# A scan and a mixture of adapters on one core: a small head for the pipeline, 2 KB rows for eight chunks, new order ranks

## The chip, the core and the metric

The kernel runs on one core of a Trainium2 chip. The metric is the device time of one execution in microseconds. The core has a matrix engine (PE, TensorE), three engines for elementwise work (DVE, ACT, POOL), a sequencer that mostly issues transfers (SP), and 16 DMA engines. Each engine works through its own list of instructions in order; semaphores join the lists.

## What is computed

The input `a` and `b` are float32 of shape 8 x 6400 x 128. For each of the 8 sequences a recurrence runs along the 6400 steps; its result `x` (51200 rows of 128) goes through a top-2 mixture of 8 low-rank adapters:

```python
for t in range(S):
    h = a[:, t] * h + b[:, t]
    out[:, t] = h
...
logits = x @ w_gate                    # 128 -> 8
topk = the two largest logits per row
w = softmax over these two
delta = sum over the two of w * (x @ A[e]) @ B[e]   # 128 -> 16 -> 128
return x + delta
```

It reads 52.4 MB and writes 26.2 MB, all in float32. The inner values are kept in float16.

## The kernel before, in words

**Chunks.** The 51200 rows are 100 chunks of 512 rows (four blocks of 128). A chunk passes through a front and a back.

The front of chunk `c`: `load` (L526) brings `a` and `b` into `a_tm` and `b_tm`, six slots of two chunks each; PE transposes both into PSUM (`A`, `B`, or `P`, which interleaves the `b` of one chunk with the `a` of the next); ACT copies `a` to `a_st` (`ae`); DVE runs the scan along 512 steps (`sc`, L613) and leaves `xT`, 128 features by 512 rows in float16. `xT` has 24 slots.

A unit `u` is a run of blocks, six of them up to the last 16 blocks, four from there on. PE multiplies each block with the eight A matrices and the gate weights side by side (`Z`, 136 columns) and ACT copies the result to `zl` (`ze`).

Units form groups. `gating(gi)` takes the logits of a group at once: maximum (`g1`, DVE), difference, mask and second maximum, sigmoid of the difference (`w1`, ACT) and the masked weights (`g8`, DVE). The five wide steps between run on POOL (`q2`, `q3`, `q5`, `q6`, `q7`), in the last six groups on DVE (`WIDE_DVE`). A group has four units, 24 blocks or six chunks; the last eight units form groups of 2, 2, 1, 1, 1, 1 (`TAPER`). There are 21 groups.

The back of a chunk needs the gates of its whole group: multiply `zl` with the gates (`mu` on POOL, or `md` on DVE for the chunks in `MU_DVE`, counted from the end), four transposes on PE (`T`), a copy out of PSUM (`te`, on DVE, on ACT for one chunk in six), then two matmuls per block that add `x` transposed back and the adapters' output (`D`), a copy to `outt` (`oe`, ACT), and the store. Stores go out for two chunks at a time, the last four for one.

**Rows of a load.** `paired(c)` (L523) chooses between two layouts. Unpaired, a partition holds four successive rows of a chunk (2 KB), and the chunk is transposed with four matmuls over all 128 partitions for each of `a` and `b`. Paired, a partition holds eight successive rows of two chunks (4 KB); each chunk then lies in one half of the partitions and takes eight transposes of 64 rows, and those of `a` and `b` alternate between the halves of the array. The first eight chunks (`HEAD`) are unpaired and come one at a time in 256 KB loads, all others are paired and come in 512 KB loads for two chunks.

**Order.** Nothing of the order is written by hand. Each operation gets a rank: a base from the number of its chunk, unit or group, plus `TEMPLATE[kind][place in the period of six]`, plus `NUDGE[name]` for single operations of the head and the tail. `Program.schedule` (L208) then plays the program with modelled durations. An engine that comes free takes, among the operations whose rank lies within `WINDOW[engine]` of its lowest, the one that could start first. The order so found is the order of the instruction list of each engine; `waits` adds the semaphores. All loads but one and all stores are in SP's list. In the model, `DMA_DEPTH` says that SP can't issue while nine transfers are under way.

**Ends.** For the last 12 chunks (`TAIL_CHUNKS`) the transposes and deltas use the PSUM banks of the front too, once its scans are done (`place`). Two stores, of chunks 56 and 78, are cut into 120 and 8 partitions (`SPLIT`).

Of the kernel before, what the change touches and what calls it, by code (L numbers as in the profile page):

```python
# [15 lines left out]
PE_FREE = 0.1  # L16
Q_RATE = {3: 3.6e-3, 5: 2.1e-3, 7: 2.1e-3}
SCAN_SELF = 0.13
ISSUE = {"sp": 0.52, "act": 0.45}
LOAD_RATE = 392e3  # L20
STORE_RATE = 408e3
# [86 lines left out]
START = (-999, "", 0)  # L108
FIRST = -9999
EARLY = -400  # L110
LEAD = []
TAPER = [2, 2, 1, 1, 1, 1]
WIDE_DVE = [1, 2, 3, 4, 5, 6]
TE_LAST = []
TAIL_UNITS = [4, 4, 4, 4]
TE_ACT = [1]
MU_DVE = [1, 2, 4, 6, 8]
TAIL_CHUNKS = 12
WARM0 = 12
WARM = 16  # L120
HALVES = 0.745
PAIR_RATE = 411e3
HEAD = 8
TAIL = 0
STORE_TAIL = [1, 1, 1, 1]
# [754 lines left out]
```

## Time and profile before

| | us |
|---|---|
| median of 3 runs | 207.19 (206.95 to 208.16) |
| the profiled execution | 207.91 |
| its span, first to last instruction | 205.9 |
| PE busy | 184.7 |
| DVE busy | 177.7 |
| ACT busy | 169.1 |
| POOL busy | 144.6 |

Busy times are sums over the span. Engine names stand before line numbers (L613 is line 613 of the kernel); a tile's name tells the step: `a_tm` and `b_tm` the loads, `pA` and `pB` the transposed inputs, `a_st` the copied `a`, `xT` the scan, `pZ` and `zl` the logits, `m`, `k`, `L`, `sd`, `g` the gate, `zw` the multiply, `zwT` its transpose, `pO` the delta, `outt` the output. A chain row or a wait row reads "waiter <- what it waited for". In a row of a stretch, the numbers are its length, then busy time and count of each engine that worked in it, the granted PE clock, the share of the DMA engines, and GB/s.

### The profile page before, as it was taken

The page shows a single profiled execution, that of the slowest core. Times are in us where ns is not written, and L with a number is a line of the kernel's source. Part 1 is how long each engine was busy: PE and PEld are TensorE (multiplying, and loading weights), DVE is VectorE, ACT ScalarE, POOL GpSimd, SP SyncE. Part 2 cuts the span into 40 slices and gives each one's busy share as a digit, 9 for nine tenths or more (in the row PEclk, how much of TensorE's full clock was granted, in tenths as well). Part 3 has the DMA queues.
Part 4 walks back from the last instruction along what each step waited for, and adds up shares of the span by engine and source line. Part 5 has one row for each costly group of instructions (what it writes and reads, how often), then busy time and mean ns, then how long its engine had stood idle before and what let it go on. Part 6 is the DMA issues. An engine that isn't in the chain of part 4 may idle for free.

```text
span 205.9 us, 7539 instructions
## 1 busy us (share of the span) xinstructions
PE 184.7 (90%) x3152; PEld 160.9 (78%) x3152; DVE 177.7 (86%) x289; ACT 169.1 (82%) x306; POOL 144.6 (70%) x176
## 2 busy tenths in 40 slices
PE   7779589999998899899799999999999999879683
PEld 6557478887897789788689888988888888857572
DVE  0789688998998899798899999999997999989881
ACT  2356668999998999899799999999999998886372
POOL 1000328879898978878788988899989898687420
PEclk9999958999999999999999999999999999999789
DMA  6999999999999999999999999999999999997388
GB/s 191 368 392 415 405 409 406 405 409 405 411 417 406 414 403 417 409 403 416 408 409 400 409 395 408 415 410 411 409 412 410 410 409 404 405 352 289 132 299 300
DMA packets 30559, 79.26 MB, mean 385 GB/s; under 512 B 3774, under 2 KB 3902, under 8 KB 30526
## 3 DMA queue, kind: packets, MB, share of 16 engines
q1 hardware_dynamic: 29054, 78.39, 97.1%
q10 hardware_dynamic: 1472, 0.40, 0.8%
q8 instruction: 25, 0.41, 0.8%
q14 instruction: 8, 0.07, 0.1%
HBM read 52.56 MB, written 26.21 MB: 383 GB/s over the span
## 4 chain that ended last, share of the span: by engine, by line
PE 67%; DVE 12%; DMA 10%; POOL 3%; issue 3%; SPq 2%; ACT 1%; DVEq 0%; POOLq 0%
PE pA L562 14%; PE pB L562 12%; PE pZ L633 11%; PE pO L734 10%; PE pO L720 10%; PE pO L735 9%; DMA a_tm<-in_a_dram 7%; DVE xT L613 5%; DMA b_tm<-in_b_dram 3%; POOL zw L707 3%; SPq L541 2%; DVE zwT L729 2%; DVE zw L711 1%; ACT outt L744 1%; DVE g L688 1%
## 5 line engine op out<-in xcount | busy, mean ns | idle before, releaser
L613 DVE TENSOR_TENSOR_SCAN xT<-a_st,xT,pB 128x512 f16<-128x512 f32 x96 | 120.3, 1253 | 9.5 <-PE pA L562 5.6
L707 POOL TENSOR_TENSOR zw<-zl,g 128x512 f16<-128x512 f32 x95 | 100.4, 1069 | 24.7 <-PE pO L720 11.3
L562 PE MATMUL pB<-ident_f,b_tm 64*128 64x64 f32 (+1 forms) x768 | 71.4, 235 | 6.5 <-DMA a_tm<-in_a_dram 2.8
L580 ACT COPY a_st<-pA 128x512 f32<-128x512 f32 x100 | 60.5, 612 | 17.5 <-PE pA L562 16.0
L562 PE MATMUL pA<-ident_f,a_tm 64*128 64x64 f32 (+1 forms) x768 | 71.7, 235 | 2.0 <-DMA a_tm<-in_a_dram 1.0
L562 PEld LDWEIGHTS pB<-ident_f,b_tm 64*128 64x128 f32 (+1 forms) x768 | 57.9, 142 | 12.5 <-issue 3.7
L562 PEld LDWEIGHTS pA<-ident_f,a_tm 64*128 64x128 f32 (+1 forms) x768 | 57.9, 142 | 8.2 <-DMA a_tm<-in_a_dram 2.3
L639 ACT COPY zl<-pZ 128x816 f32<-128x816 f32 (+1 forms) x68 | 58.0, 853 | 2.3 <-PE pZ L633 1.6
L744 ACT COPY outt<-pO 128x512 f32<-128x512 f32 x92 | 52.7, 609 | 7.7 <-PE pO L735 7.3
L734 PE MATMUL pO<-ident_h,xT 128*128 128x128 f16 x368 | 50.1, 223 | 1.2 <-DVE zwT L729 1.0
L735 PE MATMUL pO<-cst_h,zwT 128*128 128x128 f16 x368 | 48.9, 220 | 0.8 <-issue 0.8
L734 PEld LDWEIGHTS pO<-ident_h,xT 128*128 128x128 f16 x368 | 40.5, 114 | 4.8 <-DVE zwT L729 2.1
L633 PE MATMUL pZ<-cst_h,xT 128*128 128x136 f16 x400 | 36.5, 228 | 1.5 <-DVE xT L613 0.6
L735 PEld LDWEIGHTS pO<-cst_h,zwT 128*128 128x128 f16 x368 | 36.9, 100 | 0.8 <-issue 0.8
L720 PE MATMUL pO<-ident_h,zw 128*128 128x128 f16 x368 | 33.2, 221 | 2.0 <-ACT outt L744 1.3
L729 DVE COPY zwT<-pO 128x512 f16<-128x512 f16 x77 | 30.2, 410 | 3.4 <-PE pO L720 3.1
L633 PEld LDWEIGHTS pZ<-cst_h,xT 128*128 128x128 f16 x400 | 27.1, 115 | 4.4 <-DVE xT L613 1.3
L720 PEld LDWEIGHTS pO<-ident_h,zw 128*128 128x128 f16 x368 | 22.3, 98 | 6.0 <-issue 1.9
L669 POOL TENSOR_TENSOR k<-zl,m 128x192 f32<-128x192 f32 x15 | 7.8, 519 | 22.9 <-DVE m L667 22.9
L671 POOL TENSOR_SCALAR L<-k 128x192 f32<-128x192 f32 x15 | 12.9, 860 | 1.3
L613 DVE TENSOR_TENSOR_SCAN xT<-a_st,pB 128x512 f16<-128x512 f32 (+1 forms) x8 | 7.5, 939 | 4.6 <-PE pB L562 4.3
L678 POOL TENSOR_TENSOR L<-k,m 128x192 f32<-128x192 f32 x15 | 7.9, 524 | 2.8 <-DVE m L676 2.7
(41 smaller groups left out, 106.1 us busy)
## 6 DMA issues: line engine op xcount, KB each, us to landing
a_tm<-in_a_dram SPq DMA_DIRECT2D x46, 512.0 KB, 10.7
b_tm<-in_b_dram SPq DMA_DIRECT2D x46, 512.0 KB, 10.6
out_dram<-outt SPq DMA_DIRECT2D x46, 512.0 KB, 10.8
a_tm<-in_a_dram SPq DMA_DIRECT2D x8, 256.0 KB, 5.8
b_tm<-in_b_dram SPq DMA_DIRECT2D x7, 256.0 KB, 6.0
out_dram<-outt SPq DMA_DIRECT2D x4, 256.0 KB, 2.7
out_dram<-outt SPq DMA_DIRECT2D x2, 480.0 KB
b_tm<-in_b_dram ACTq DMA_DIRECT2D x1, 256.0 KB, 3.6
```

The source lines that it names most:

```text
L562: last = eng["pe"].transpose(*args)
L580: lambda: eng["act"].copy(a_st[c % NA][:, :], pA[:, c % 2, :]), fr(c, "ae"))
L613: last = eng["dve"].tensor_tensor_scan(out=x[:, s0:s1], data0=a_st[c % NA][:, s0:s1], data1=pB[:, c % 2, s0:s1], initial=init, op0=ALU.mul ...
L633: last = eng["pe"].matmul(pZ[:, k // (n // 2), o : o + W], xblock(b0 + k), Awg_h)
L639: return eng["act"].copy(zl[:, zb : zb + n, :].rearrange("p (h k) w -> p h (k w)", h=2), pZ[:, :, 0 : n // 2 * W])
L671: lambda e: e.tensor_scalar(out=ll, in0=kk, scalar1=0.0, scalar2=-1.0e30, op0=ALU.is_ge, op1=ALU.mult), dve=not main)
L707: lambda: eng["pool"].tensor_tensor(out=wv, in0=zv, in1=gv, op=ALU.mult), ba(gi, c, "mu"))
L720: last = eng["pe"].transpose(ptile[:, k * 128 : k * 128 + 128], zw[w][:, k, :], ident_h[:, :])
L729: lambda: eng["dve"].tensor_copy(zwT[w][:, :], ptile[:, 0:C]), ba(gi, c, "te"))
L734: eng["pe"].matmul(dst, xblock(b0 + k), ident_h[:, :], start=True, stop=False)
L735: last = eng["pe"].matmul(dst, zwT[w][:, k * 128 : k * 128 + 128], B_h, start=False, stop=True)
L744: lambda: eng["act"].copy(outt[:, o0 : o0 + n, :].rearrange("p k w -> p (k w)"), bank),
```

## The change

- The first three units are four blocks long, one chunk each (`HEAD_UNITS`), and the groups begin with one of one unit and one of two (`LEAD`). So the gate of chunk 0 needs chunk 0 alone, that of chunks 1 and 2 needs these two, and the groups of six chunks begin with chunk 3.
- At the end one of the two groups of two units goes (`TAPER`). There are 22 groups; the sixth from the end, whose wide steps run on DVE, now is one of 24 blocks.
- Chunks 4 to 11 (pairs 2 to 5, `FLAT`) are loaded two at a time in unpaired rows of 2 KB and transposed over 128 partitions. Chunks 0 to 3 still come one at a time (`HEAD` 4). Before, chunks 4 to 7 were single unpaired loads and 8 to 11 paired.
- The multiplies of the last ten chunks all run on DVE (`MU_DVE`, before five of the last eight), and the PSUM copies `te` of six of the last ten on ACT (`TE_LAST`).
- No store is cut (`SPLIT` is empty).
- In the planner, an operation that waits for a landing, or that is issued by SP, counts its operands as later by a margin when the order is sought (`LAND_MARGIN`, `SP_MARGIN`). Its transfer rates are changed by about 1%, and the windows, the templates and the nudges are all new.

```diff
+SP_MARGIN = 2.0
+LAND_MARGIN = 1.0
...
-LOAD_RATE = 392e3
-STORE_RATE = 408e3
+LOAD_RATE = 387e3
+STORE_RATE = 413e3
...
 NUDGE = {
-    "A0": -158.252, "A1": -127.324, "A2": -123.096, "A3": 32.941, "A4": 44.278, "A5": 34.44, "A6": 59.414, "A7":
...
+    "A0": -7.373, "A1": 6.112, "A10": -1.64, "A11": 34.468, "A12": 1.111, "A2": 15.408, "A3": -24.636, "A4":
...
-WINDOW = {'pe': 16.262, 'act': 17.153, 'dve': 47.02, 'pool': 47.064, 'sp': 57.831}
+WINDOW = {'pe': 42.345, 'act': 35.431, 'dve': 24.751, 'pool': 5.955, 'sp': 63.924}
...
-LEAD = []
-TAPER = [2, 2, 1, 1, 1, 1]
+LEAD = [1, 2]
+TAPER = [2, 1, 1, 1, 1]
 WIDE_DVE = [1, 2, 3, 4, 5, 6]
-TE_LAST = []
+TE_LAST = [1, 2, 4, 6, 8, 10]
 TAIL_UNITS = [4, 4, 4, 4]
+HEAD_UNITS = [4, 4, 4]
+FLAT = [2, 3, 4, 5]
 TE_ACT = [1]
-MU_DVE = [1, 2, 4, 6, 8]
+MU_DVE = [1, 2, 3, 4, 5, 6, 7, 8, 9, 10]
...
-PAIR_RATE = 411e3
-HEAD = 8
+PAIR_RATE = 414.5e3
+HEAD = 4
 TAIL = 0
 STORE_TAIL = [1, 1, 1, 1]
-SPLIT = {56: [120, 8], 78: [120, 8]}
+SPLIT = {}
 TEMPLATE = {
...
-    "sc": [-2.149, -1.286, 6.521, -19.69, -9.638, -0.216],
+    "sc": [-11.65, -1.923, -9.807, -8.205, -4.3, 4.861],
...
-    "oe": [26.926, 32.894, 33.316, 36.556, 35.829, 26.06],
+    "oe": [19.127, 13.522, 10.649, 2.757, 11.757, 27.623],
...
+    def margin(self, d, op):
+        return (SP_MARGIN if op.eng == "sp" else 0.0) + (LAND_MARGIN if d.sem is not None else 0.0)
+
     def schedule(self):
...
-                users[d.i].append((op, self.lag(d, op)))
+                users[d.i].append((op, self.lag(d, op) + self.margin(d, op)))
...
-    for n in [U] * ((NBLK - sum(TAIL_UNITS)) // U) + TAIL_UNITS:
+    for n in HEAD_UNITS + [U] * ((NBLK - sum(HEAD_UNITS) - sum(TAIL_UNITS)) // U) + TAIL_UNITS:
...
         def un(u, kind):
-            return (PERIOD * (u // GMAX), kind, u % GMAX)
+            v = u - len(HEAD_UNITS)
+            if v < 0:
+                return ((units[u][0] + units[u][1] - 1) // J - 1, kind, 0)
+            return (sum(HEAD_UNITS) // J + PERIOD * (v // GMAX), kind, v % GMAX)
...
         def paired(c):
-            return HEAD <= c < NCH - TAIL
+            return HEAD <= c < NCH - TAIL and c // HC not in FLAT
...
-                    q, f"{key}{c}", n * C * D * 4 / (PAIR_RATE if paired(c) else LOAD_RATE),
+                    q, f"{key}{c}", n * C * D * 4 / (PAIR_RATE if paired(c) else STORE_RATE if n == HC else LOAD_RATE),
```

More of the change, by code (lines that the diff above doesn't have):

```diff
@@ L121 @@
 HALVES = 0.745
-PAIR_RATE = 411e3
-HEAD = 8
+PAIR_RATE = 414.5e3
+HEAD = 4
 TAIL = 0
 STORE_TAIL = [1, 1, 1, 1]
-SPLIT = {56: [120, 8], 78: [120, 8]}
+SPLIT = {}
 TEMPLATE = {
-    "la": [-13.284, -13.376, -10.147],
-    "lb": [-12.856, -11.393, -13.112],
-    "A": [3.619, 4.619, -4.264, 6.619, 7.619, 8.619],
-    "B": [-2.245, 2.718, -8.407, 8.99, 6.061, 4.41],
-    "ae": [-1.493, 12.357, 10.831, 7.96, 5.931, 11.772],
-    "sc": [-2.149, -1.286, 6.521, -19.69, -9.638, -0.216],
-    "Z": [6.623, 2.916, -2.696, 9.959],
-    "ze": [6.413, 12.686, 18.636, 4.611],
-    "g1": [1.078],
-    "g2": [15.192],
-    "g3": [12.311],
-    "g4": [-7.624],
-    "g5": [43.586],
-    "g6": [18.91],
-    "w1": [27.261],
+    "la": [-7.837, -6.512, -2.793],
+    "lb": [-6.969, -4.142, -2.441],
+    "A": [-29.85, -22.77, -4.07, -28.889, -8.078, -19.823],
+    "B": [-12.19, -0.608, 4.625, 4.731, 6.492, -13.789],
+    "ae": [13.823, -17.155, -11.299, -7.863, -15.554, -16.07],
+    "sc": [-11.65, -1.923, -9.807, -8.205, -4.3, 4.861],
+    "Z": [-11.931, -1.652, 0.404, 0.668],
+    "ze": [-0.53, 2.002, 2.058, 7.184],
+    "g1": [-5.254],
+    "g2": [6.652],
+    "g3": [-1.394],
+    "g4": [5.837],
+    "g5": [2.097],
+    "g6": [-3.795],
+    "w1": [9.977],
     "w2": [27.183],
@@ L146 @@
     "p3": [35.473],
-    "mu": [22.377, 11.789, 38.051, -6.995, 25.901, 25.822],
-    "T": [17.564, 18.694, 15.643, 19.013, 20.568, 20.925],
-    "te": [11.47, 21.167, 12.791, -1.785, 1.996, 11.732],
-    "D": [13.525, 17.402, 15.169, 14.035, 19.652, 27.901],
-    "oe": [26.926, 32.894, 33.316, 36.556, 35.829, 26.06],
-    "st": [25.679, 26.621, 29.881],
-    "ta": [14.725, 30.746, 16.943, 18.052, 19.161, 20.27],
-    "md": [78.718, -0.018, -87.87, 12.1, 13.209, 14.318],
+    "mu": [7.135, 7.159, 9.752, 13.89, 13.317, 14.36],
+    "T": [8.957, 2.123, 1.909, 11.496, 1.102, -5.077],
+    "te": [5.714, 2.101, 13.025, 13.738, 15.827, 9.439],
+    "D": [11.989, 5.151, 4.181, 3.366, 5.179, -2.649],
+    "oe": [19.127, 13.522, 10.649, 2.757, 11.757, 27.623],
+    "st": [27.717, 29.832, 33.435],
+    "ta": [-17.067, 3.889, 6.417, 53.389, -5.208, -15.308],
+    "md": [14.061, -2.161, 18.001, 16.54, -9.981, -19.458],
     "wu": [-0.198],
-    "ch": [26.813],
+    "ch": [4.744],
     "mb": [0.0],
-    "q2": [17.668],
-    "q3": [-16.399],
-    "q5": [-0.842],
-    "q6": [-2.93],
-    "q7": [1.928],
+    "q2": [-2.296],
+    "q3": [2.325],
+    "q5": [0.245],
+    "q6": [3.55],
+    "q7": [1.073],
     "q8": [35.473],
-    "g7": [47.426],
-    "g8": [9.111],
+    "g7": [-1.33],
+    "g8": [-0.424],
 }
@@ L721, in tr @@
                 return last
-            o_T[c] = P.add("pe", f"T{c}", 0.1 + 0.056 * n, [(o_mu[c], True), (o_ih, True)] + free + [(o, True) for o in o_wu if c < 2], tr, ba(gi, c, "T"))
+            o_T[c] = P.add("pe", f"T{c}", 0.1 + 0.056 * n, [(o_mu[c], True), (o_ih, True)] + free + [(o, True) for o in (o_wu if c < 2 else [])], tr, ba(gi, c, "T"))
             if te_act(c):
```

147 rows, old and new, of the table NUDGE are left out of this document.

## The prediction

> **What bounds the kernel now.** I read the page first, for busy shares and DMA slices.
>
> ```profile
> span 205.9 us, 7539 instructions
> PE 184.7 (90%) x3152; PEld 160.9 (78%) x3152; DVE 177.7 (86%) x289; ACT 169.1 (82%) x306; POOL 144.6 (70%) x176
> GB/s 191 368 392 415 405 409 406 405 409 405 411 417 406 414 403 417 409 403 416 408 409 400 409 395 408 415 410 411 409 412 410 410 409 404 405 352 289 132 299 300
> DMA packets 30559, 79.26 MB, mean 385 GB/s; under 512 B 3774, under 2 KB 3902, under 8 KB 30526
> ```
>
> No engine stands out, and the transfers run flat at about 410 GB/s except at both ends. So the run has three stages. The view by stretches cuts it where the first store is issued (38 us) and where the loads have ended (176 us); the second table is the same view for the tile `outt`, whose ACT copies are the finished chunks.
>
> ```profile
> 0.00:38.00 38.00, 30.62 (x376) 25.48 (x376) 26.58 (x28) 22.70 (x37) 10.28 (x18) 0.91 0.98 371
> 38.00:176.00 138.00, 132.47 (x2485) 117.08 (x2484) 128.33 (x188) 128.66 (x234) 120.90 (x147) 1.00 1.03 409
> 176.00:206.00 30.00, 21.66 (x300) 18.35 (x298) 22.84 (x75) 17.70 (x37) 13.45 (x13) 0.94 0.78 291
> ...
> 0.00:38.00 38.00, 1.08 (x2) 0.91 0.98 371
> 38.00:176.00 138.00, 43.53 (x77) 1.00 1.03 409
> 176.00:206.00 30.00, 12.48 (x22) 0.94 0.78 291
> ```
>
> At 409 GB/s the 79.26 MB take 193.8 us. The span is 12.1 us longer: 38 x (1 - 371/409) = 3.5 us go at the front and 30 x (1 - 291/409) = 8.6 us at the end. Those 8.6 us are all that can be won cheaply. In the middle 77 chunks come out in 138 us, 1.79 each. (The copies add to 101, since one lies across 38 us.) After 176 us the last 22 need until 203.05, the end of the last row below: 27.05 us or 1.23 each, though a store of 262 KB needs 0.64. The tail thus waits for chunks, not for transfers. Why 22 are left shows in the order of time: SP, then the page's row on how long a load takes to land (10.6 us), DVE, and ACT (its first row, two copies from 36.5 us, is the view of `outt` up to 40 us).
>
> ```profile
> 38.18 0.40 SPq L779 DMA_DIRECT2D out_dram<-outt  x1
> 161.92 0.47 SPq L541 DMA_DIRECT2D b_tm<-in_b_dram  x1
> 162.44 40.97 SPq L779 DMA_DIRECT2D out_dram<-outt  x23
> ...
> b_tm<-in_b_dram SPq DMA_DIRECT2D x46, 512.0 KB, 10.6
> ...
> 6.03 1.22 DVE L613 TENSOR_TENSOR_SCAN xT<-a_st,pB 128x512 f16<-128x512 f32 x1 [4.30 <-PE pB L562]
> 22.85 0.35 DVE L667 TENSOR_REDUCE m<-zl 128x24 f32<-128x192 f32 x1 [0.42 <-ACT zl L639]
> 30.66 0.33 DVE L688 SCALAR_TENSOR_TENSOR g<-L,sd 128x192 f32<-128x192 f32 x1
> 185.34 1.27 DVE L613 TENSOR_TENSOR_SCAN xT<-a_st,xT,pB 128x512 f16<-128x512 f32 x1
> 186.53 0.40 DVE L729 COPY zwT<-pO 128x512 f16<-128x512 f16 x1
> ...
> L744 ACT COPY outt<-pO x2: 586/618/650, 36.5 to 37.6; 128x512 f32<-128x512 f32 x2
> 201.88 1.17 ACT L744 COPY outt<-pB 128x512 f32<-128x512 f32 x2 [1.11 <-PE pB L735]
> ```
>
> The first scan runs at 6 us, the first gate only from 22.85 to 31.0, and the first chunk is out at 37.1. So the outputs start 31 us behind the scans, and at the end 22 of them are still to come when the last load, issued at 161.92, has landed (about 172.5). POOL is busy 10.28 of the first 38 us, and PE falls idle and is then slowed (granted clock 0.66 for ten microseconds):
>
> ```profile
> 20.00:25.00 5.00, 2.76 (x60) 2.33 (x60) 2.96 (x4) 2.87 (x5) 1.54 (x3) 1.00 1.02 405
> 25.00:35.00 10.00, 9.12 (x128) 7.65 (x124) 8.50 (x11) 7.86 (x14) 5.20 (x8) 0.66 1.03 408
> ```
>
> **The change part by part.** Prices (instruction groups by form):
>
> ```profile
> L707 POOL TENSOR_TENSOR zw<-zl,g 128x512 f16<-128x512 f32 x95 | 100.4, 1069 | 24.7 <-PE pO L720 11.3 <-DVE g L688 6.2 <-PE pB L720 4.0
> L711 DVE TENSOR_TENSOR zw<-zl,g 128x512 f16<-128x512 f32 x5 | 3.3, 682 | 0.0
> L729 DVE COPY zwT<-pO 128x512 f16<-128x512 f16 x77 | 30.2, 410 | 3.4 <-PE pO L720 3.1
> L726 ACT COPY zwT<-pO 128x512 f16<-128x512 f16 x15 | 9.2, 614 | 0.4 <-PE pO L720 0.4
> L671 POOL TENSOR_SCALAR L<-k 128x192 f32<-128x192 f32 x15 | 12.9, 860 | 1.3
> L674 DVE TENSOR_TENSOR L<-L,k 128x32 f32<-128x32 f32 x4 | 0.6, 190 | 0.0
> L674 DVE TENSOR_TENSOR L<-L,k 128x96 f32<-128x96 f32 x2 | 0.5, 250 | 0.0
> L680 DVE TENSOR_TENSOR k<-k,L 128x32 f32<-128x32 f32 x4 | 1.4, 403 | 0.0
> L688 DVE SCALAR_TENSOR_TENSOR g<-L,sd 128x96 f32<-128x96 f32 x2 | 1.2, 609 | 0.0
> L562 PE MATMUL pA<-ident_f,a_tm 64*128 64x64 f32 x736 | 66.3, 232 | 1.0 <-issue 0.9
> L562 PE MATMUL pA<-ident_f,a_tm 128*128 128x128 f32 x32 | 5.3, 298 | 1.0 <-DMA a_tm<-in_a_dram 1.0
> ```
>
> *Lead groups (1 and 2 units of one chunk).* Chunk 0 no longer waits for chunks 1 to 5. From its scan (7.25) its chain is logits and their copy (about 1 us), eight gate steps, multiply 1.07, transpose, copy 0.41, delta, copy 0.6. Small gate steps on POOL have no row; five of them lie between 5 x 0.19 (the DVE twin on 32 elements) and 5 x 0.86 (POOL on 192). I take 1.5 us in all, near the small end because the tile is small. That puts chunk 0 out at about 16 us, chunks 1 and 2 by 20, and the first store near 20 instead of 38. The next group, chunks 3 to 8, can be gated once chunk 8 is scanned: the first three slices (15.4 us) move 4.9 MB, which are nine chunks of 0.52 MB, and with landing and scan I take 20 us. With the present 8 us of gate and 6 us from gate to output it comes out from about 35 us, where chunk 3 now comes at 37.1 + 3 x 1.79 = 42.5. That is 7.5 us, about four chunks at 1.79. The extra gate work on DVE, about 1.6 us for two small groups (0.17 to 0.40 a step), falls into a front in which DVE is busy 26.58 of 38 us.
>
> *What four chunks are worth.* They leave the tail at its pace of 1.23: **-4.9 us**. Two stores moved ahead of the loads delay the last load by 4 x 0.64 = 2.6 us. That is hidden, since the last load lands about 13 us before its chunk is scanned (185.34); without that cover it would cost 2.6.
>
> *End of the list.* Five more multiplies go from POOL to DVE: 5 x (0.68 - 0.08) = +3.0 us of DVE; the 0.08 is what successive DVE rows overlap (the scan at 185.34 ends at 186.61, the copy behind it starts at 186.53). Six PSUM copies go to ACT: -6 x (0.41 - 0.08) = -2.0. One 24-block group gets its five wide steps on DVE (about 0.35 each on 192 elements, continuing 190 and 250 ns: +1.8), and one 12-block group goes (seven steps of about 0.25 and one of 0.61, -2.4). Net **+0.4** on DVE, which is busy 22.84 us of the 26 in which it still works; POOL gives up five multiplies and five wide steps, ACT takes 6 x 0.61 in slack (17.70 of 30).
>
> Rows of this kernel show DVE steps held up while POOL multiplies: L680 takes 403 ns where its twin L674 takes 190, L688 609 on 96 elements. So each of the five moved multiplies costs between 0 and one POOL multiply more, 5 x 1.07 = 5.3 us in all. I keep 0: the nearest row is that of the five multiplies that DVE has now, 682 ns, with nothing held up in it. The Trainium skill (SBUF — State Buffer, "Who interferes with whom") says that a DVE instruction with two SBUF inputs and a GpSimd instruction that reads SBUF exclude each other for a whole instruction. By that rule a multiply that starts beside POOL waits; the trace agrees in L680 and not in L711.
>
> *2 KB rows for chunks 4 to 11.* Four chunks (8 to 11) change from 64-row to 128-row transposes. The half-height ones run in pairs, a beside b: 66.3/92 = 0.72 us a chunk; the full ones 2 x 5.3/8 = 1.33. So +2.4 us of PE at most, at 16 to 24 us, where PE idles 2.2 us of 5 and waits for loads; cost 0, bounds 0 and 2.4. Chunks 4 to 7 come as one 512 KB load instead of two: chunk 4 lands perhaps 1 us later, chunk 8 as before; nothing behind it.
>
> *No split stores.*
>
> ```profile
> out_dram<-outt SPq DMA_DIRECT2D x2, 480.0 KB
> out_dram<-outt SPq DMA_DIRECT2D x2, 32.0 KB
> ```
>
> Two stores were cut into 480 and 32 KB; whole they cost two issues fewer. A cut moves work among DMA engines, and no row here tells the engines apart: between 0 and one 512 KB transfer time (1.28 us) of the slowest engine, for the one cut store that stands ahead of the last loads. I take half, **+0.6**. The Trainium skill (DMA: Bandwidth & Descriptors, "Why a DMA increments its semaphore by 16 and not by 1") says a DMA uses the largest count up to 16 that divides its outer dimension, so 120 rows spare one engine. By it the spared engine gets the full 1.28 back and the sum would be 204.0; no row here shows it.
>
> *New ranks.* The order of every engine is replanned. In the templates the mean place of `oe` less that of `sc` falls from 31.9 + 4.4 = 36.3 to 14.2 + 5.2 = 19.4 chunks, so outputs are planned nearer to their scans. Below: nothing beyond the four chunks. Above: nine chunks, if the real distance (about 20 chunks) shrinks in proportion, 5 x 1.23 = 6.2 us more, which the transfers don't allow. I take nothing.
>
> Sum: -4.9 + 0.4 + 0.6 = **-3.9 us**. The profiled execution took 207.91 us for its span of 205.9, the median is 207.19, 1.29 over the span. Span 202.0, median **203.3**. The floor is 193.8 + 3.5 for the front + 2.3 for the last store to land (the shortest of the stores after 176 us):
>
> ```profile
> L779 SPq DMA_DIRECT2D out_dram<-outt x15: 333/372/1120, 175.7 to 203.1; - x15
> ...
> DMA to landing us min/median/max: 2.3/3.5/11.3
> ```
>
> That is 199.6 of span, 200.9 of median.
>
> **The rivals.** *Same:* the tail is DVE's own chain (gate, multiply, copy, chunk after chunk), and the chunks saved at the front only lengthen the waits. Then the 4.9 go, +0.4 and +0.6 stay, and perhaps the clock dip is saved (10 x 0.34 = 3.4 us of PE at most, half of it felt): 206.5. For it: DVE busy 22.84 of 26 us; against it: 22 chunks were left over for it to do.
>
> *Held multiplies:* the moved multiplies and POOL's take turns, half of the 5.3 us bound: 203.3 + 2.7 = 206.0. For it L680's 403 ns; against it L711's 682, and that POOL has fewer multiplies left to collide with.
>
> *Slower:* the steady stage. With half the planned distance between a scan and its output, PE, which works in order, reaches transposes and deltas before their operands are there.
>
> ```profile
> L734 PE MATMUL pO<-ident_h,xT 128*128 128x128 f16 x304 | 40.6, 222 | 0.1
> L720 PE MATMUL pO<-ident_h,zw 128*128 128x128 f16 x311 | 27.7, 220 | 0.8 <-POOL zw L707 0.5 <-ACT outt L744 0.2
> ```
>
> Today these wait 0.9 us in the whole middle stage, for some 77 chunks, and PE is busy 132.47 of 138. At x us a chunk more PE loses 77x: from x = 0.05 the gain of 3.9 is gone, and at 0.1 it is 203.3 + 7.7 = 211.0. Against it: a chunk's transfers (0.79 MB) take 1.92 us at 409 GB/s, more than the 1.79 of the chunks, so part of such waits would hide behind them.
>
> *The early stores don't come early:* SP issues in order, and DMA is full at the front; a store that the new order puts behind the same loads goes out no sooner than now: 207.2.
>
> **How the numbers follow.** Forecast 0.58, same 0.12, held multiplies 0.08, slower 0.18, no early stores 0.04. A measurement of this kernel can tell about 1%, 2.1 us. The forecast's own range is 200.9 to 205.1; chances are faster 0.58, within 1% 0.24 (the three cases between 206.0 and 207.2), slower 0.18. The low end is the floor; the high end, 209.8, takes in the three cases near no change with the cover of 2.6 us lost (207.2 + 2.6), and leaves out most of the slower case, some 0.15.
>
> **What would show it.** Right: the first store issued near 20 us, POOL at work by 12, no clock dip at 25 to 35; fewer than 19 `outt` copies after the loads' end; the tail's rate over 291 GB/s. The wrong way: DMA slices under 400 GB/s before 170 us, `outt` copies over 1.9 us apart, or PE waits on `zw` and `zwT` of several microseconds. A last scan later than 188 us would mean that the delayed loads lost their cover.

## The result and the profile after

The changed kernel takes 204.19 us (median of 4 runs, 204.05 to 204.35); the kernel before takes 207.07 beside it (4 runs, 206.02 to 208.16). The ratio is 0.9858, 95% interval 0.9824 to 0.9893: 1.4% faster, 2.9 us. The forecast was 203.3. All times of whole kernels are medians of fast executions; one of the four of the last kernel below (214.22 us) was slow and is left out. The page of the changed kernel, its busy shares and its GB/s in 40 slices:

```profile
span 202.4 us, 7462 instructions
PE 182.1 (90%) x3120; PEld 157.8 (78%) x3120; DVE 176.2 (87%) x291; ACT 172.6 (85%) x314; POOL 139.0 (69%) x176
GB/s 186 365 387 390 407 410 406 402 412 406 406 415 410 410 410 411 417 409 407 411 414 405 411 408 417 408 411 416 406 413 412 411 414 410 404 401 373 347 359 149
```

The middle is as flat as before. The last slices no longer fall to 132; they go 401, 373, 347, 359. The view by stretches, cut where the prediction cut it, with the same view for the tile `outt` behind the dots:

```profile
0.00:38.00 38.00, 33.16 (x408) 28.49 (x409) 28.57 (x39) 26.27 (x46) 16.99 (x33) 1.00 0.99 367
38.00:176.00 138.00, 130.06 (x2444) 114.24 (x2441) 128.06 (x186) 127.62 (x231) 117.76 (x140) 1.00 1.03 410
176.00:202.40 26.40, 18.88 (x273) 15.10 (x272) 19.59 (x68) 18.75 (x40) 4.20 (x4) 0.97 0.87 329
...
38.00:176.00 138.00, 45.09 (x76) 1.00 1.03 410
176.00:202.40 26.40, 10.94 (x20) 0.97 0.87 329
```

Before, the last stretch of the same view, cut at that span's own end, was:

```profile
176.00:205.90 29.90, 21.66 (x300) 18.35 (x298) 22.84 (x75) 17.70 (x37) 13.45 (x13) 0.94 0.78 292
```

Measured against 410 GB/s, the transfers lose 38 x (1 - 367/410) = 4.0 us at the front (before 3.6) and 26.4 x (1 - 329/410) = 5.2 us at the end (before 29.9 x (1 - 292/410) = 8.6). So the gain lies in the end stage: 3.4 us less idle of the transfers, of 3.5 us of span. Up to 176 us both kernels move the same bytes to within 0.1 MB: 0.15 MB fewer at the front, 0.14 more in the middle. Twenty copies are left in place of 22.

The order of time, SP, DVE and ACT:

```profile
30.35 0.40 SPq L784 DMA_DIRECT2D out_dram<-outt  x1
164.21 0.59 SPq L546 DMA_DIRECT2D b_tm<-in_b_dram  x1
164.83 34.74 SPq L784 DMA_DIRECT2D out_dram<-outt  x20
...
12.29 0.27 DVE L489 CAST cst_h<-cst_f 128x264 f16<-128x264 f32 x1
13.73 0.19 DVE L672 TENSOR_REDUCE m<-zl 128x4 f32<-128x32 f32 x1 [1.17 <-ACT zl L644]
14.01 0.24 POOL L674 TENSOR_TENSOR k<-zl,m 128x32 f32<-128x32 f32 x1 [12.54 <-DVE m L672]
181.32 1.27 DVE L618 TENSOR_TENSOR_SCAN xT<-a_st,xT,pB 128x512 f16<-128x512 f32 x1
...
20.62 0.59 ACT L749 COPY outt<-pO 128x512 f32<-128x512 f32 x1
27.73 0.63 ACT L749 COPY outt<-pO 128x512 f32<-128x512 f32 x1
35.06 0.61 ACT L749 COPY outt<-pO 128x512 f32<-128x512 f32 x1
197.80 0.58 ACT L749 COPY outt<-pA 128x512 f32<-128x512 f32 x1
```

The first gate starts at 13.73 us (before 22.85), the first chunk is out at 21.2 (before 37.1), the first store goes at 30.35 (before 38.18) and the last load 2.3 us later than before. The last scan comes 4 us earlier.

### The profile page after: what moved, and what is told of

The parts are those of the page before. It is cut to its first block, busy times and chain, and to the rows that moved or that the text cites. A ratio compares the mean times of both kernels' runs of the same rounds, so it can differ in the third digit from the quotient of the medians.

```text
span 202.4 us, 7462 instructions
## 1 busy us (share of the span) xinstructions
PE 182.1 (90%) x3120; PEld 157.8 (78%) x3120; DVE 176.2 (87%) x291; ACT 172.6 (85%) x314; POOL 139.0 (69%) x176
## 4 chain that ended last, share of the span: by engine, by line
PE 23%; DMA 20%; DVE 19%; issue 1%; ACT 1%; SPq 0%; DVEq 0%
DMA b_tm<-in_b_dram 13%; DVE xT L618 9%; DMA a_tm<-in_a_dram 7%; PE pA L567 5%; PE pZ L638 4%; PE pB L567 4%; PE pO L725 3%; PE pO L739 3%; DVE zwT L734 3%; PE pO L740 3%; DVE zw L716 3%; DVE g L693 1%; ACT zwT L731 1%; ACT outt L749 1%; DVE m L672 1%
## 5 line engine op out<-in xcount | busy, mean ns | idle before, releaser
L712 POOL TENSOR_TENSOR zw<-zl,g 128x512 f16<-128x512 f32 x90 | 94.1, 1061 | 16.2 <-DVE g L693 11.3
L567 PE MATMUL pA<-ident_f,a_tm 64*128 64x64 f32 (+1 forms) x752 | 68.7, 233 | 4.0 <-DMA b_tm<-in_b_dram 2.5
L567 PE MATMUL pB<-ident_f,b_tm 64*128 64x64 f32 (+1 forms) x752 | 68.6, 232 | 2.1 <-DMA a_tm<-in_a_dram 1.1
L567 PEld LDWEIGHTS pA<-ident_f,a_tm 64*128 64x128 f32 (+1 forms) x752 | 55.8, 139 | 10.0 <-DMA b_tm<-in_b_dram 3.3
L567 PEld LDWEIGHTS pB<-ident_f,b_tm 64*128 64x128 f32 (+1 forms) x752 | 55.4, 139 | 7.1 <-DMA a_tm<-in_a_dram 1.6
L740 PEld LDWEIGHTS pO<-cst_h,zwT 128*128 128x128 f16 x368 | 36.5, 99 | 0.5 <-issue 0.5
L725 PE MATMUL pO<-ident_h,zw 128*128 128x128 f16 x368 | 35.2, 220 | 1.2 <-ACT outt L749 0.4
L638 PEld LDWEIGHTS pZ<-cst_h,xT 128*128 128x128 f16 x400 | 26.4, 115 | 8.6 <-DVE xT L618 5.3
L725 PEld LDWEIGHTS pO<-ident_h,zw 128*128 128x128 f16 x368 | 22.6, 97 | 5.2 <-issue 1.3
L674 POOL TENSOR_TENSOR k<-zl,m 128x192 f32<-128x192 f32 (+2 forms) x16 | 7.8, 490 | 14.4 <-DVE m L672 14.4
L683 POOL TENSOR_TENSOR L<-k,m 128x192 f32<-128x192 f32 (+2 forms) x16 | 7.8, 489 | 9.6 <-DVE m L681 9.6
L676 POOL TENSOR_SCALAR L<-k 128x192 f32<-128x192 f32 (+2 forms) x16 | 12.8, 799 | 1.4
L731 ACT COPY zwT<-pO 128x512 f16<-128x512 f16 x16 | 9.6, 602 | 3.4 <-PE pO L725 3.4
```

The costliest lines, as they stand in the source:

```text
L567: last = eng["pe"].transpose(*args)
L638: last = eng["pe"].matmul(pZ[:, k // (n // 2), o : o + W], xblock(b0 + k), Awg_h)
L676: lambda e: e.tensor_scalar(out=ll, in0=kk, scalar1=0.0, scalar2=-1.0e30, op0=ALU.is_ge, op1=ALU.mult), dve=not main)
L712: lambda: eng["pool"].tensor_tensor(out=wv, in0=zv, in1=gv, op=ALU.mult), ba(gi, c, "mu"))
L725: last = eng["pe"].transpose(ptile[:, k * 128 : k * 128 + 128], zw[w][:, k, :], ident_h[:, :])
L740: last = eng["pe"].matmul(dst, zwT[w][:, k * 128 : k * 128 + 128], B_h, start=False, stop=True)
```

## The experiments

They come in three groups: parts changed with the order kept; parts undone with the order replanned from the ranks the kernel has; and parts undone with ranks searched anew. The theory at the start was the prediction's: the lead groups bring outputs forward, so fewer chunks are left when the loads end.

### Whole stores in the kernel before

```diff
-SPLIT = {56: [120, 8], 78: [120, 8]}
+SPLIT = {}
```

> The kernel before with the two cut stores whole, nothing else; the order of every engine is the same. The prediction's +0.6 for the whole stores means 207.7 against 207.1 (bounds 0 and +1.3). The rival, that landed loads wait 3 to 12 us for their scan and so hide it, means 207.1, no difference.

Measured: 207.34 us against 207.09, ratio 1.0009 (0.9986 to 1.0031).

### Cut stores in the kernel after

```diff
-SPLIT = {}
+SPLIT = {56: [120, 8], 78: [120, 8]}
```

> The changed kernel with stores 56 and 78 cut again, same order. If whole stores cost 0.6, this is 203.6. In the changed kernel loads land only 1 to 4 us ahead of their scan from 90 us on, so if a late DMA engine matters at all it matters here: up to 1.3 less, 202.9. The rival, nothing to it: 204.2.

Measured: 204.56 us, ratio to the kernel before 0.9887 (0.9867 to 0.9907). The two runs agree: the cut is worth nothing that shows. Whole stores cost +0.2 with zero inside the interval, and cutting them again gains nothing.

### The late gate and the old dealing, planned with the ranks there are

In the first, the gate of group 0 also waits for the scan of chunk 9, so the early start is gone (the loop lists the loads and fronts of these chunks ahead of that gate):

```diff
-            ... [(o_ze[u], True) for u in range(u0, u0 + n)] + old,
+            ... [(o_ze[u], True) for u in range(u0, u0 + n)] + old + ([(o_sc[9], True)] if gi == 0 else []),
...
+            while gi == 0 and nf < 10:
+                load_next(nf)
+                front(nf)
+                nf += 1
```

> The changed kernel, but the first gate also waits for the scan of chunk 9 (about 22 us), the time at which the kernel before gates first; ranks the same, order planned anew. Theory (the gain is the early start): the outputs start some 8 us later, about four chunks, and of the 2.9 us gained most go: 206.3 to 207.5. Rival (the gain is the new dealing of the last chunks and the new ranks): 204.0 to 205.0.

Measured: 226.44 us, ratio 1.0937 (1.0895 to 1.098). In the second, the work of the last chunks is dealt to the engines as before:

```diff
-TE_LAST = [1, 2, 4, 6, 8, 10]
+TE_LAST = []
-MU_DVE = [1, 2, 3, 4, 5, 6, 7, 8, 9, 10]
+MU_DVE = [1, 2, 4, 6, 8]
```

> The changed kernel with the multiplies and PSUM copies of the last chunks dealt as before (five multiplies on DVE, no copy on ACT), planned anew with the ranks that exist. By the prediction's sum the new dealing costs DVE 3.0 - 2.0 = +1.0, so undoing it gives 203.2 to 204.2. Rival (POOL's five multiplies held up the end, which the changed trace speaks for: its POOL stops at 183 us instead of 198): 205.2 to 206.7.

Measured: 231.27 us, ratio 1.116 (1.1123 to 1.1197). Both are misses of both theories. The page's GB/s row of the second:

```profile
GB/s 204 381 388 398 410 407 403 411 407 410 409 409 412 409 417 412 407 409 413 405 412 413 409 414 412 411 410 411 413 412 405 364 162 122 0 3 91 152 276 216
```

Up to the 31st slice it is the row of a good kernel; then the transfers stand still for two slices of 5.7 us. The edit touches ten chunks by less than 1 us each, but the replanned lists of the engines no longer fit each other. So these two runs price an order and not the part; with ranks searched anew, below, the same two edits stand at 208.99 and 208.16. Some 20 us hang on ranks that fit the plan, and a part can only be judged with ranks of its own.

### Half of the loads

From chunk 12 on, only half the rows of each load are read, with the same issues in the same order. It leaves out 23 MB of transfers; where rows are not read, the scan works on what the tile held before, so these two kernels serve for their times alone.

```diff
+                    if c >= 12:
+                        view, dst = view[:, 0:J, :], dst[:, 0:J, :]
```

> The changed kernel with only the first half of each partition's rows loaded from chunk 12 on, so 23 MB (some 56 us of transfer time) are left out and those chunks compute on old rows; the orders of all engines stay. Theory: from 50 us on this kernel waits for its loads (they land 1 to 4 us ahead of their scan), so the middle quickens to what the engines can do: 198 to 201. Rival: the order itself sets the pace and the transfers only look full: 203.5 to 204.5.

> The same half loads in the kernel before. Its loads land 5 to 12 us ahead of their scan until 90 us and its tail waits for chunks, so by the theory it gains little: 205.5 to 207. If transfers hold this kernel too, it gains as much as the changed one: 201 to 204.

Measured: after 200.02 us (ratio to before 0.9656, 0.9594 to 0.9718), 4.2 us off; before 201.62 (0.9734, 0.9666 to 0.9802), 5.5 us off, where 205.5 to 207 was expected. So transfers hold both kernels, not the changed one alone. Of the 2.9 us between the two, 1.6 stay when the loads are light. And though 23 MB are 56 us of transfers at 410 GB/s, only 4.2 and 5.5 us come off, and the transfers then run at means of 284 and 281 GB/s. So something else holds these two kernels at 200 us, presumably the engines' own lists.

### Ranks searched anew: control, late gate, old dealing, 4 KB rows

Each kernel got its own list of ranks, one per operation, and its own windows. Random changes of single ranks were kept when the kernel's own planner ended its plan earlier. These four had the same length of search, each from the changed kernel's ranks. The first changes nothing else and is the control. The diff leaves out the numbers.

```diff
-            rank[op.i] = op.base + (TEMPLATE[op.kind][op.k] if op.kind in TEMPLATE else 0.0) + NUDGE.get(op.name, 0.0)
+            rank[op.i] = RANKS[op.i]
```

> The changed kernel with nothing but its ranks searched anew from those it has: the same 1329 steps and the same cuts, another order beside the loads and stores. It is the control of the next three, whose ranks are searched anew in the same way, so that an undone part is not charged with ranks that no longer fit. If the gain of the change sits in its parts (first gate early, end dealt anew), any well fitted order keeps it: 203 to 206 us. If it sits in the one list of ranks that the change brought, another list loses it: 207 or more, and a list that does not fit at all would stand where the two failed runs stood, 226 to 231.

Control: 204.64 us, ratio to before 0.987 (0.9838 to 0.9902). The gain does not sit in the one list of ranks.

> The first gate waits for the scan of chunk 9 again, with ranks searched anew for that. Theory of the early start (the outputs run four chunks ahead, 4 x 1.12 us at the end's pace, 3.4 us less idle of the transfers at the end): 3 to 5 us above the control run. Rival, the loads bound the middle and the end takes up a late start: within 1 us of the control.

The late gate, with the edit shown above: 208.99 us, ratio 1.0102 (1.007 to 1.0134), 4.35 above the control. The early start's theory had 3 to 5, its rival less than 1. But this kernel has its first output at 31.3 us, where the kernel before has it at 36.5, and it has the new dealing too, and still it is 1.0% slower than the kernel before. So part of the 4.35 belongs to the searched list and not to the gate.

> Only five of the last chunks' multiplies on VectorE and none of the last rounded copies (the dealing of before), with ranks searched anew for that. Theory of the early start: the dealing is worth nothing or up to 1 us, so at most 1 us above the control. Rival, the dealing at the end is what freed it (GpSimd, 5 multiplies more of 1.9 us, ends last): 2 to 5 us above the control.

The old dealing, with the edit shown above: 208.16 us, ratio 1.0027 (1.0002 to 1.0053), 3.5 above the control. This is the rival's range, and against my theory. But its front had slipped too (first output at 30.6 us, control 24.1; three chunks out at 38 us, control five), so it does not yet price the dealing.

> Chunks 4 to 11 in 4 KB rows with the 120-row transposes again, with ranks searched anew for that. The prediction's value for this part, 0: within 1 us of the control. Its upper bound, read the other way (the 2 KB rows let the first gates come early): up to 2.4 us above the control; if the shorter rows cost transfer time, 0.5 to 1 us below it.

```diff
-FLAT = [2, 3, 4, 5]
+FLAT = []
```

4 KB rows for chunks 4 to 11: 204.17 us, ratio 0.9852 (0.9819 to 0.9886), 0.5 below the control. The "120-row transposes" of the expectation should read 64-row; and chunks 4 to 7, which before came one at a time, are paired here too. The 0.5 lies within the 1 us of the prediction's value and at the edge of the other reading (0.5 to 1 us below); the two ratios differ by 0.2%, with 0.3% of uncertainty each, so the 2 KB rows bring or cost nothing that shows. This run also says something of the front: its first output comes at 29.9 us, 6 us behind the control's, and costs nothing. The time of the first output alone is thus not what the early start is worth; four chunks are out at 38 us here, five in the control.

### The old dealing behind an unchanged front, and both parts undone

> The dealing of before at the end once more, but now with the control run's order kept as it is up to about 140 us and only the ranks behind that searched anew, because the run with the old dealing had also let its front slip (first output at 30.6 us in place of 24.1). If the dealing itself costs the 3.5 us that that run lost, this one stands 2.5 to 4 us above the control (204.6), at 207 to 208.6. If the loss came from the slipped front, it is within 1 us of the control, 205.6 at most.

The order is that of the control up to about 130 us on SP and 140 us elsewhere; the ranks behind that were searched from the control's, and longer than in the other runs. Measured: 207.47 us, ratio 0.9998 (0.9976 to 1.002), 2.8 above the control (2.7 by the two ratios). The slipped front was not the cause of that loss.

> Both parts undone in one kernel, the late first gate and the old dealing, with ranks searched anew. If the two gains add, as the prediction's sum has its terms do, 4.3 + 3.5 us above the control: about 212.5. If the end waits for whichever of the two is late (the outputs that are left, or the multiplies that GpSimd has left), so that either alone brings nothing, it stands where each of the two stood: 208 to 210. It also tells how far the search of ranks by itself is from the ranks of the kernel before (207.3), which has the same two parts.

Both undone: 210.15 us (209.56 to 212.21), ratio 1.0137 (1.0061 to 1.0212). By the ratios that is 2.7% above the control, where the two prices, 2.3% and 1.3%, would add to 3.6%. That is between the 212.5 of gains that add and the 208 to 210 of gains that don't, just above the second. With 0.8% of uncertainty each way, whether they add stays open.

The run also gives a bound on the method. This kernel has the late start and the old dealing that the kernel before has, and stands 1.4%, or 2.8 us, above it. Searched lists can thus be worse than tuned ones by about that much, and the 4.35 and the 2.8 are prices under searched ranks that may hold a part of it. The whole change gains 2.9 us, so the 4.35 must hold some of it. Taken off in full, the 2.8 leaves 1.5 us of the early start's price and nothing of the dealing's. That these searches found no list that keeps the gain with either part undone is shown; that none exists is not.

What these runs share is in the view by stretches: the last stretch and, behind the dots, the same stretch for `outt`. Control, late gate, old dealing with the front kept, both undone:

```profile
176.00:202.50 26.50, 18.67 (x277) 15.08 (x274) 19.50 (x68) 18.48 (x40) 4.22 (x5) 0.96 0.86 325
...
176.00:202.50 26.50, 10.88 (x20) 0.96 0.86 325
```

```profile
176.00:206.70 30.70, 22.75 (x340) 18.47 (x337) 24.10 (x76) 22.58 (x46) 9.30 (x9) 0.99 0.75 283
...
176.00:206.70 30.70, 12.25 (x22) 0.99 0.75 283
```

```profile
176.00:205.50 29.50, 20.27 (x304) 16.71 (x301) 22.50 (x74) 18.34 (x38) 12.16 (x12) 0.96 0.79 295
...
176.00:205.50 29.50, 11.77 (x21) 0.96 0.79 295
```

```profile
176.00:208.30 32.30, 23.94 (x364) 19.68 (x359) 24.67 (x76) 20.27 (x41) 14.25 (x14) 0.99 0.73 272
...
176.00:208.30 32.30, 13.18 (x24) 0.99 0.73 272
```

| kernel | `outt` copies from 176 us on | us per copy, up to the end of the last | length of the stretch | idle of the transfers in it |
|---|---|---|---|---|
| after | 20 | 1.12 | 26.4 | 5.2 |
| control | 20 | 1.11 | 26.5 | 5.5 |
| 4 KB rows | 20 | 1.17 | 26.2 | 5.5 |
| old dealing, front kept | 21 | 1.19 | 29.5 | 8.3 |
| old dealing, front slipped | 22 | 1.16 | 29.9 | 8.5 |
| before | 22 | 1.23 | 29.9 | 8.6 |
| late gate | 22 | 1.22 | 30.7 | 9.5 |
| both undone | 24 | 1.16 | 32.3 | 10.9 |

All eight run their transfers at 409 or 410 GB/s from 38 to 176 us. They part in the last column, and it follows the first. The pace does not follow the dealing: the late gate has the new dealing and 1.22, both undone has the old one and 1.16. The row with 21 stands out: one chunk more, but 2.8 us more idle than the control. Its GpSimd (POOL) shows where. Timeline of POOL from 175 us, old dealing with the front kept:

```profile
179.39 2.20 POOL L773 TENSOR_TENSOR zw<-zl,g 128x512 f16<-128x512 f32 x2 [2.02 <-PE pO L786]
182.58 2.08 POOL L773 TENSOR_TENSOR zw<-zl,g 128x512 f16<-128x512 f32 x2 [1.00 <-DVE g L754]
185.12 2.08 POOL L773 TENSOR_TENSOR zw<-zl,g 128x512 f16<-128x512 f32 x2 [0.46 <-PE pO L786]
188.40 1.06 POOL L773 TENSOR_TENSOR zw<-zl,g 128x512 f16<-128x512 f32 x1 [1.21 <-PE pO L786]
190.84 1.06 POOL L773 TENSOR_TENSOR zw<-zl,g 128x512 f16<-128x512 f32 x1 [1.38 <-PE pO L786]
...
194.76 1.06 POOL L773 TENSOR_TENSOR zw<-zl,g 128x512 f16<-128x512 f32 x1 [1.06 <-DVE g L754]
```

and the control's, whose POOL is done at 182.94:

```profile
177.95 1.06 POOL L773 TENSOR_TENSOR zw<-zl,g 128x512 f16<-128x512 f32 x1 [1.89 <-PE pO L786]
179.84 3.10 POOL L773 TENSOR_TENSOR zw<-zl,g 128x512 f16<-128x512 f32 x3 [0.83 <-DVE g L754]
```

A late multiply on POOL takes 1.06 us, and before it POOL mostly waits 0.5 to 2 us, for the transposes of an earlier product (L786) or for the gate. On DVE it takes 0.69 and needs no hand-over from DVE's own gate. I take that chain, and not POOL's busy time (12.16 of 29.5 us), to be what the old dealing leaves at the end; it is read from these rows and not tested by itself. How the 2.8 us divide between the multiplies, the copies moved to ACT and the searched list was not tried either.

## Why the prediction was right, and where only the sum was

**The bound** (8.6 us of idle transfers at the end are all that can be won cheaply) is right: the gain is 3.4 us of them. The profile of before at 207.91 lies 0.8 above its median, so 3.5 us of span are 2.9 of median. The span was forecast 202.0 and came out at 202.4. The other half of the 0.9 us miss is the step from span to median, taken as 1.29 and measured as 204.19 - 202.4 = 1.8.

**Lead groups.** Chunk 3 out "from about 35 us": 35.7. Chunk 0 out at 16 was wrong: 21.2. The five small steps on POOL, estimated between 0.19 and 0.86 us, took 0.24 to 0.33. What failed was the start. The logits need the weights cast to float16 (L489 in the DVE rows above), and that cast runs at 12.29, behind the scans of the first chunks in DVE's list; the prediction's chain from the scan did not have it. From the gate's start to the output it took 7.5 us, about what the prediction left for it. The first store came at 30.35 and not near 20, since a store takes two chunks and chunk 1 was out at 28.4 (forecast by 20; its group's gate ran only from 17.95 to 22.6).

**Four chunks, -4.9 us.** This is the term that was mis-sized. The lead came as forecast at the front and then grew, but most of it did not reach the end. Copies of `outt` that have ended:

| by | before | after | lead |
|---|---|---|---|
| 38 us | 1 | 5 | 4 |
| 100 us | 33 | 40 | 7 |
| 140 us | 57 | 62 | 5 |
| 176 us | 78 | 80 | 2 |

Up to 176 us both kernels move the same bytes, so what is stored earlier stands against loads that come later. The delay of the last load (forecast 2.6, measured 2.3) was called hidden because loads landed 13 us ahead of their scan. They no longer do. In the waits of the changed kernel from 38 to 176 us PE now waits for loads, all of it after 100 us, where the lead begins to shrink; the kernel before has no such row in this stretch:

```profile
PEld pA L567 <- DMA b_tm<-in_b_dram: 3.3, 4, 1.2
...
PE pA L567 <- DMA b_tm<-in_b_dram: 2.5, 3, 1.0
```

So the step that failed is the one from four chunks ahead at the front to four fewer left at the end: there it is two, 2 x 1.23 = -2.5. With half of the loads the changed kernel has the same 40 out by 100 us and 83 in place of 80 by 176, so loads do hold it there. But the kernel before gains three as well (81), so that the loads alone took the lead is argued and not shown.

**End of the list, +0.4.** The end goes faster, not slower: the last 20 chunks take (198.38 - 176)/20 = 1.12 us each, not 1.23, which is 20 x 0.11 = -2.2 us. The prediction counted DVE's busy time, where the moved work costs 0.4, and neither the chain of gate, multiply and transpose that the dealing shortens nor the steps that it frees (next part). That the faster pace comes from the dealing is not shown: undoing the dealing alone cost 2.8 with the front kept, of which up to 2.8 can be the searched list, and the late gate lost the pace with the new dealing in place. DVE did become full. The stretches of 6 us from 176 on, before and then after (busy time of DVE is the third pair):

```profile
176.00:182.00 6.00, 5.06 (x85) 4.41 (x84) 5.46 (x19) 4.95 (x11) 3.99 (x5) 1.00 1.04 397
182.00:188.00 6.00, 5.10 (x71) 3.94 (x68) 5.45 (x16) 4.46 (x9) 4.75 (x6) 1.00 0.87 321
188.00:194.00 6.00, 3.88 (x58) 3.47 (x57) 6.00 (x18) 2.08 (x6) 3.65 (x3) 0.94 0.56 212
```

```profile
176.00:182.00 6.00, 5.20 (x89) 4.47 (x89) 6.00 (x15) 4.50 (x11) 3.41 (x4) 1.00 1.06 404
182.00:188.00 6.00, 5.66 (x83) 4.60 (x80) 6.00 (x23) 5.33 (x12) 0.80 (x1) 1.00 0.98 378
188.00:194.00 6.00, 5.03 (x75) 4.03 (x73) 5.93 (x30) 5.04 (x12) 0.00 (x0) 1.00 0.86 324
```

DVE is busy 17.93 of 18 us, before 16.91. The rival *same* (the tail is DVE's own chain) thus names what looks like the present limit, but not the result: DVE now works 19.59 us for the last 20 copies, before 22.84 for 22.

**Held multiplies, kept at 0.** Right, and more: the ten multiplies ran unhindered and the steps that had been held are free. By form, after:

```profile
L716 DVE TENSOR_TENSOR zw<-zl,g 128x512 f16<-128x512 f32 x10 | 6.8, 686 | 0.0
L693 DVE SCALAR_TENSOR_TENSOR g<-L,sd 128x32 f32<-128x32 f32 x5 | 0.9, 189 | 0.3 <-ACT sd L687 0.3
L685 DVE TENSOR_TENSOR k<-k,L 128x32 f32<-128x32 f32 x4 | 0.8, 191 | 0.0
```

The mean of 403 ns for the four small `k` before hides one long step: one takes 1.05 us from 189.99 on, beside multiplies on POOL (189.90 to 192.55), the other three about 0.19. A small `g` took 1.04 us there too, at 191.56. POOL now stops at 182.8, and none of them is long. That is 4 x 0.21 = 0.85 us of DVE for `k` and about as much for `g` (399 ns before, 188 at the end now), which the prediction, looking only for new holds, did not credit. In these rows the rule it cited from the Trainium skill (SBUF — State Buffer, "Who interferes with whom") and the trace agree: no multiply on POOL beside them, no hold.

**2 KB rows** 0, **no cut stores** +0.6: the first is right as far as can be told (204.17 without them), the second was +0.2 with zero in its interval. The other value that the prediction gave for it, 1.28 us by a rule of the Trainium skill (DMA: Bandwidth & Descriptors, "Why a DMA increments its semaphore by 16 and not by 1"), is not seen in either direction.

**New ranks** 0: as a choice among fitting lists it is right (204.64 with another), as a statement about ranks it was too light, as the runs at 226 and 231 show.

**Not in the sum.** From the last copy to the end of the span it is 202.4 - 198.38 = 4.0 us, before 2.85: +1.2. So the measured terms are -2.5 - 2.2 + 1.2 = -3.5 us of span, near the forecast's -3.9 with other parts. This is bookkeeping of one stretch and adds up by construction; it is not a price of causes. That the total came so near is in part luck: the early start's term was twice too large, and a pace that was forecast to be a little slower made up for it.

**The signs.** The clock's dip is gone, as forecast. From 25 to 35 us PE is busy more and at full clock:

```profile
20.00:25.00 5.00, 4.51 (x56) 3.87 (x55) 4.22 (x6) 4.30 (x8) 2.69 (x5) 1.00 1.02 406
25.00:35.00 10.00, 9.43 (x178) 7.82 (x176) 9.82 (x14) 9.13 (x17) 7.29 (x10) 1.00 1.03 408
```

The rate of the tail (329 GB/s, over 291) held. The other signs were missed: POOL began at 14.0 (forecast by 12), the first store went at 30.35 (near 20), and 20 copies were left where fewer than 19 were asked for. None of the signs of the slower case appeared: the slices from 20 to 170 us stay above 400 (the four ahead of them reach 390 at most; before, the fourth had 415), the 76 copies of the middle come 1.82 us apart on average, the last scan is at 181.32 and not later than 188, and no PE wait on `zw` or `zwT` in the middle is of several microseconds.

## What to carry to other kernels

A lead won at the front can be gone before it counts: here it was seven chunks at 100 us and two when the loads had ended, so count what is still ahead there and not at the start. At a pipeline's end, follow the chain of one chunk through the engines; here the busy time of the engine that received the work had the wrong sign. And undoing one part of a kernel whose order is planned needs a control with ranks searched in the same way, or the run prices a broken order; and how far the search falls short has to be measured too, since here it was as large as one of the prices.

## What the runs showed of the hardware that was not expected

PE stands still in the kernel before with no wait that the profile can name ("issue"), 3.7 us in the middle. Waits from 38 to 176 us, before:

```profile
PE pB L562 <- issue: 2.0, 3, 1.0
...
PE pA L562 <- issue: 0.9, 1, 0.9
PE pO L735 <- issue: 0.8, 2, 0.6
```

and three of the rows of the timeline:

```profile
71.78 0.27 PE L562 MATMUL pB<-ident_f,b_tm 64*128 64x64 f32 x1 [0.79 <-issue]
86.19 0.27 PE L562 MATMUL pA<-ident_f,a_tm 64*128 64x64 f32 x1 [0.90 <-issue]
100.55 0.27 PE L562 MATMUL pB<-ident_f,b_tm 64*128 64x64 f32 x1 [1.00 <-issue]
```

The kernel before with whole stores has them again (1.8, 1.2 and 0.9). With half of the loads 0.3 is left, in the changed kernel 0.4:

```profile
PE pB L564 <- issue: 0.3, 1, 0.3
```

```profile
PE pO L739 <- issue: 0.4, 1, 0.4
```

Instructions arrive by a DMA queue of their own, which is on the profile page of the changed kernel and, the same, of the kernel before:

```profile
q8 instruction: 25, 0.41, 0.8%
```

The trace of the kernel before has the times of these packets of 16 KB. They end at 62.5, 70.4, 84.9, 91.3 and 99.1 us, and five of PE's six stops end at 63.9, 71.8, 86.2, 92.7 and 100.6, each 1.3 to 1.4 us behind one. The kernel with whole stores shows the same five, 1.4 to 1.6 us behind a packet, and the one stop of the changed kernel ends 1.2 us behind one (167.5 and 168.8). So these stops end a nearly fixed time behind a packet of instructions, as they would if PE waited for it; a sixth stop, of 0.24 us, has no packet close before it. With half of the loads the five are gone; one of 0.3 us is left that does not stand in this relation. That full transfers are what makes these packets late fits the runs with half of the loads, but is argued and not shown. Why the gaps are smaller in the changed kernel stays open too; the 2 KB rows alone are not the reason, since they stay small without them (0.7). They cannot be the gain, since the middle moves 409 and 410 GB/s with and without them.
